# Attention, MLP and gated MLP on one core: each engine's queue laid down by the kernel's own list scheduler

## The chip, the cores and the metric

The kernel runs on one core of one Trainium2 chip. The metric is the time of one execution on the device in microseconds; what is reported is the median of several runs.

## What is computed

Sparse attention in which each query keeps its 32 largest scores, then an MLP with SiLU, then a gated product with two more matrices. In the reference:

```python
scores = scale * np.matmul(q, k.transpose(0, 1, 3, 2))          # 4 x 8 heads, 576 x 576, head_dim 64
kth = np.partition(scores, -top_k, axis=-1)[..., -top_k:-top_k + 1]   # top_k = 32
scores = np.where(scores >= kth, scores, -1000000000.0)
attn = softmax(scores)                                          # max subtracted, sum + 1e-9
x = (attn @ v) as 2304 tokens x 512
h = x @ w_in;  x = (h * sigmoid(h)) @ w_out                     # d_ff 2048
out = ((x @ w1) * (x @ w2)) @ w3 @ w_out2                       # d_ff 1024, out 2304 x 512
```

## The kernel before

The 2304 tokens are cut into 6 blocks of 384 (BLOCKS). Block j has 8 heads of 3 tiles of 128 queries, 24 tiles, which are taken in pairs. For a pair, `plan_scores` makes the scores on TensorE in two halves of 288 columns (L397, L398) and copies them to SBUF on ScalarE (L401). `plan_topk` finds the 32 largest of a row on VectorE by four MAX8 (L428) and three MATCH_REPLACE8 (L432), and masks (L448) and exponentiates (L454) on ScalarE. `plan_av` transposes the probabilities by TensorE (L538, L540; in blocks 0 and 1, which are "native", by a matmul with a diagonal matrix, L535), copies them on ScalarE (L546, L553, L554) and multiplies with v (L566 native, L575). For float32 accuracy at the speed of fp32r, most operands are split into a high part (a ScalarE cast) and a low part (a GpSimd subtraction), and every MLP product is three matmuls (`three`, L637 to L639).

`mlp(j)` has 16 steps of the first MLP (`l1`, `tanh`, `gate`, `split_to`, `l2`), then 8 steps of the gated one (`l3`, `prod`, `l4`, L758). w3 times the last matrix is folded once at the beginning (`fold_steps`, L220 and L225). The weights come as 64-bit numbers; 24 pieces of the fold and 48 of the MLPs are loaded (`convert_load`, L121 and L123), converted by two ScalarE passes (L128, L129), a GpSimd clamp (L132) and a VectorE shift (L137), split (L183, L184) and written to DRAM (L172) while block 0 is computed. Blocks 1 to 5 stream them back (`stream`, L188). The raw pieces have 4 buffers.

The order in which operations are recorded comes from a plan in ticks, 7 of them (SLOT) for each pair, into which `Spread` deals the steps of `mlp(j)`, so that MLP j runs beside attention j+1. The framework then orders the queues by a simulated timeline of its own (`schedule_with_timeline_sim=True`, at the launch), from that recorded order as priority. The eight PSUM banks are eight fixed tiles; `bank` pops one from a list at recording, and `done` puts it back, so that an operation is tied to one bank when it is recorded:

```python
free_banks = [ps_p.tile([128, 512], FP32, name=f"bank{i}") for i in range(8)]
def bank(why=""):
    b = free_banks.pop(0)
    held[id(b)] = why
    return b
```

Of the kernel before, what the change touches and what calls it, by code (L numbers as in the profile page):

```python
# [1 line left out]

# [21 lines left out]
LAG = 1  # L24
WT = 3
# [4 lines left out]
XB = 6  # L30
GB = 2
# [18 lines left out]
TB = 2  # L50


@with_exitstack
def attention_moe_moe2_kernel(
    ctx: ExitStack,
# [9 lines left out]
    w4: bass.AP,  # L65
    out: bass.AP,
):
    nc = tc.nc
    B, H, D2, S = qT.shape
    D = D2 // 2  # L70
    NT, DM = out.shape
# [8 lines left out]
    scale = 1.0 / float(D) ** 0.5  # L80
    NB = len(BLOCKS)

    w4_p = ctx.enter_context(tc.tile_pool(name="w4", bufs=1))
    wt_p = ctx.enter_context(tc.tile_pool(name="wt", bufs=WT))
    raw_p = ctx.enter_context(tc.tile_pool(name="raw", bufs=2))
    x_p = ctx.enter_context(tc.tile_pool(name="x", bufs=XB))
    x2_p = ctx.enter_context(tc.tile_pool(name="x2", bufs=1))
    g_p = ctx.enter_context(tc.tile_pool(name="g", bufs=GB + LAG))
    kv_p = ctx.enter_context(tc.tile_pool(name="kv", bufs=2))
    s_p = ctx.enter_context(tc.tile_pool(name="s", bufs=2))  # L90
    pt_p = ctx.enter_context(tc.tile_pool(name="pt", bufs=2))
    ps_p = ctx.enter_context(tc.tile_pool(name="ps", bufs=1, space=bass.MemoryType.PSUM))
    dram = ctx.enter_context(tc.tile_pool(name="dram", bufs=1, space=bass.MemoryType.DRAM))


    free_banks = [ps_p.tile([128, 512], FP32, name=f"bank{i}") for i in range(8)]

    held = {}

    def bank(why=""):  # L100
        if not free_banks:
            raise RuntimeError(f"no bank: {sorted(held.values())}")
        b = free_banks.pop(0)
        held[id(b)] = why
        return b

    def done(b):
        held.pop(id(b))
        free_banks.append(b)
# [80 lines left out]
    def fold_steps():  # L190
# [89 lines left out]
    ready = [0] * NB  # L280
# [97 lines left out]
    def plan_scores(n, base):  # L378
# [9 lines left out]
        def go(tick, j, h, i, half, si, r0, r1):  # L388
            hd = heads[j, h]
            if n not in tiles:  # L390
                tiles[n] = s_p.tile([128, 2, S], FP32, tag="st", bufs=SB, name="st")
            m = pairs[n].index((j, h, i))
            kk = hd["k"][si][0]
            ps = bank("s")
            cs = slice(half * HS, (half + 1) * HS)
            q_ = hd["q"][:, i * 128:(i + 1) * 128]
            nc.tensor.matmul(ps[:, 0:HS], lhsT=q_, rhs=kk[:, 0, cs], start=True, stop=False)  # L397
            nc.tensor.matmul(ps[:, 0:HS], lhsT=q_, rhs=kk[:, 1, cs], start=False, stop=True)  # L398

# [103 lines left out]
    def plan_av(j, h):  # L503
# [22 lines left out]
        for kc in range(KC):  # L526
            u = {}

            def tr(u=u, kc=kc):
                u["ps"] = ps = bank("pt")  # L530
                for i in range(BLOCKS[j]):
                    p = st["p"][i]
                    if native:
                        kn = REM if kc == NFULL else 128
                        nc.tensor.matmul(ps[0:kn, i * 128:(i + 1) * 128], lhsT=p[:, kc * 128:kc * 128 + kn],  # L535
                                         rhs=st["d"][:, i * 128:(i + 1) * 128], start=True, stop=True)
                    elif kc < NFULL:
                        nc.tensor.transpose(ps[:, i * 128:(i + 1) * 128], p[:, kc * 128:kc * 128 + 128], ident)  # L538
                    else:
                        nc.tensor.transpose(ps[:, i * 128:(i + 1) * 128], p[:, kc * 128:kc * 128 + 128], ident)  # L540

            def ev(u=u, kc=kc):
                if native:
                    kn = REM if kc == NFULL else 128
                    pf = pt_p.tile([128, T], FP32, tag="ph", bufs=3, name="pn")
                    nc.scalar.copy(out=pf[0:kn], in_=u["ps"][0:kn, 0:T])  # L546
                    done(u["ps"])
                    u["m"] = pf
                    return
# [264 lines left out]
            self.i = len(self.todo)  # L814

    with ExitStack():
        make_identity(nc, ident)
        nc.gpsimd.memset(sums, 1e-9)
        nc.gpsimd.memset(low, 7.5 * 2.0 ** -16 - 0.5)
        start = min(plan)  # L820
        fs = fold_steps() + [f for k in range(8) for f in (lambda k=k: conv_step(k), lambda: None)]
        side = Spread(fs, ready[0] - RO)
        j = -1
        tick = start
        while plan or j + 1 < NB:
            todo = plan.pop(tick, [])
            while todo:
                todo.sort(key=lambda x: x[:2])
                todo.pop(0)[2]()
                todo += plan.pop(tick, [])  # L830
            if tick >= FS:
                side.tick()
            if j + 1 < NB and tick == ready[j + 1]:
                side.rest()
                j += 1
                side = Spread(mlp(j), ready[j + 1] - ready[j] - MO if j + 1 < NB else 1)
            tick += 1
        side.rest()


# [42 lines left out]
```

## Time and profile before

| | |
|---|---|
| median of 3 runs | 1192.65 us (1192.61 to 1194.92) |
| profiled execution | 1192.3 us, span 1190.2 us |
| instructions | 19686 |
| TensorE busy, matmuls | 1114.8 us (94%) |
| TensorE busy, weight loads | 994.6 us (84%) |
| VectorE, ScalarE, GpSimd busy | 905.4, 860.0, 712.9 us |
| DMA | 273.53 MB, 230 GB/s |
| mean granted TensorE clock | 0.974 |

Busy time is the union of an engine's instructions. TensorE's matmuls overlap one another in the record, so its share says less than that of the other engines. In the tables below, PE is TensorE's matmuls, PEld its weight loads, DVE VectorE, ACT ScalarE, POOL GpSimd, SP the engine whose queue issues most DMAs; L12 is line 12 of the kernel.

### The profile page before, as it was taken

The numbers are of one execution on the slowest core, as the hardware profiler recorded it, in microseconds if no ns is written. First come the engines' busy times: TensorE is split into PE (matmuls) and PEld (weight loads), VectorE is DVE, ScalarE is ACT, GpSimd is POOL, SyncE is SP. The second block draws the span as 40 slices with busy tenths as digits, with TensorE's granted clock in tenths as the row PEclk, the third lists the DMA queues.
The fourth block names the chain that finished last, engine by engine and source line by source line (L and its number), as shares of the span: only waits on it lengthen the run. The fifth ranks groups of instructions, "written<-read, shape, count | busy, mean of one in ns | idle before, by whom it ended". The sixth has DMA issues, their size and how long they took to land.

```text
span 1190.2 us, 19686 instructions
## 1 busy us (share of the span) xinstructions
PE 1114.8 (94%) x6216; PEld 994.6 (84%) x6216; DVE 905.4 (76%) x2112; ACT 860.0 (72%) x1931; POOL 712.9 (60%) x744
## 2 busy tenths in 40 slices
PE   5899958989789999999999999999999999999998
PEld 2454547888679899999899999999999999999997
DVE  6999899787857888999889987887799899601100
ACT  6896888888887587887778877877868778642221
POOL 4443465777767366786677866767855766542231
PEclk8999978999889999999999999999999999999999
DMA  9965395786978567756688776889757774538640
GB/s 295 323 205 167 105 319 170 273 308 233 313 254 273 205 219 242 227 201 236 204 249 277 239 243 206 282 281 316 249 200 227 231 249 154 188 113 284 243 166 26
DMA packets 127879, 273.53 MB, mean 230 GB/s; under 512 B 40480, under 2 KB 65056, under 8 KB 127776
## 3 DMA queue, kind: packets, MB, share of 16 engines
q1 hardware_dynamic: 119712, 245.02, 62.7%
q10 hardware_dynamic: 8064, 27.27, 6.0%
q8 instruction: 49, 0.80, 0.3%
q14 instruction: 54, 0.44, 0.1%
HBM read 216.14 MB, written 56.10 MB: 229 GB/s over the span
## 4 chain that ended last, share of the span: by engine, by line
PE 68%; ACT 11%; DVE 10%; DMA 6%; issue 3%; POOL 3%; SPq 0%; ACTq 0%; POOLq 0%; DVEq 0%
PE bank L637 14%; PE bank L638 14%; PE bank L639 13%; PE bank L758 8%; DVE top L428 4%; PE bank L575 4%; DVE wk L432 3%; PE bank L538 3%; DMA raw<-in_w_dram 3%; PE bank L397 2%; PE bank L566 2%; PE bank L398 2%; PE bank L535 2%; PE bank L220 2%; DVE w L137 2%
## 5 line engine op out<-in xcount | busy, mean ns | idle before, releaser
L428 DVE MAX8 top<-wk 128x8 f32<-128x576 f32 x432 | 320.3, 752 | 5.2
L652 POOL TENSOR_TENSOR gl<-gf,gh 128x384 fp32r<-128x384 f32 x144 | 148.9, 1036 | 139.6 <-ACT gh L651 138.4
L432 DVE MATCH_REPLACE8 wk<-top,wk 128x576 f32<-128x576 f32 x288 | 213.2, 742 | 0.0
L556 POOL TENSOR_TENSOR pl<-pf,ph 128x384 fp32r<-128x384 f32 x128 | 129.5, 1020 | 78.1 <-ACT ph L554 69.4
L401 ACT ACTIVATE st<-bank 128x288 f32<-128x288 f32 (+1 forms) x320 | 127.8, 415 | 32.4 <-PE bank L398 29.9
L428 DVE MAX8 top<-st 128x8 f32<-128x576 f32 x144 | 108.0, 751 | 46.5 <-ACT st L401 46.0
L637 PE MATMUL bank<-x2h,wt 128*128 128x384 f32 x384 | 131.5, 346 | 6.1 <-ACT x2h L696 4.6
L638 PE MATMUL bank<-gl,wt 128*128 128x384 f32 x384 | 132.3, 344 | 1.7 <-POOL gl L652 1.2
L637 PE MATMUL bank<-xh,wt 128*128 128x384 f32 x384 | 131.0, 344 | 2.9 <-DVE gf L679 2.0
L638 PE MATMUL bank<-x2l,wt 128*128 128x384 f32 x384 | 130.2, 339 | 1.1 <-POOL x2l L697 0.9
L639 PE MATMUL bank<-gh,wt 128*128 128x384 f32 x384 | 130.2, 339 | 0.0
L639 PE MATMUL bank<-xh,wt 128*128 128x384 f32 x384 | 129.9, 338 | 0.0
L638 PE MATMUL bank<-xl,wt 128*128 128x384 f32 x384 | 129.8, 338 | 0.0
L639 PE MATMUL bank<-x2h,wt 128*128 128x384 f32 x384 | 129.3, 337 | 0.0
L397 PE MATMUL bank<-kk,qs 128*128 128x288 f32 x320 | 108.3, 350 | 18.3 <-POOL qs L320 5.1
L679 DVE SCALAR_TENSOR_TENSOR gf<-th,bank 128x384 f32<-128x384 f32 x96 | 52.2, 549 | 88.3 <-ACT th L674 84.3
L448 ACT ACTIVATE e<-st,nt 128x576 f32<-128x576 f32 x144 | 105.1, 775 | 14.1 <-DVE nt L440 12.9
L454 ACT ACTIVATE e<-e,nb 128x576 f32<-128x576 f32 x144 | 112.0, 780 | 0.1
L651 ACT CAST gh<-gf 128x384 fp32r<-128x384 f32 x144 | 74.1, 516 | 49.6 <-DVE gf L746 33.0
L432 DVE MATCH_REPLACE8 wk<-top,st 128x576 f32<-128x576 f32 x144 | 106.7, 742 | 0.0
L553 ACT COPY pf<-bank 128x384 f32<-128x384 f32 (+1 forms) x160 | 77.3, 483 | 32.5 <-PE bank L538 20.5
L132 POOL TENSOR_SCALAR t<-t 128x512 int16<-128x512 int16 x72 | 59.1, 820 | 67.8 <-ACT t L128 58.2
(90 smaller groups left out, 2924.3 us busy)
## 6 DMA issues: line engine op xcount, KB each, us to landing
wt<-scr SPq DMA_DIRECT2D x240, 512.0 KB, 4.3
scr<-wt ACTq DMA_DIRECT2D x48, 512.0 KB, 5.4
k<-kk SPq DMA_DIRECT2D x32, 576.0 KB, 5.2
kk<-k SPq DMA_DIRECT2D x32, 576.0 KB, 5.1
raw<-in_w_dram SPq DMA_DIRECT2D x24, 512.0 KB, 5.6
kr<-in_kT_dram SPq DMA_DIRECT2D x32, 288.0 KB, 5.5
raw<-in_w3T_dram SPq DMA_DIRECT2D x16, 512.0 KB, 5.2
raw<-in_w_in_dram SPq DMA_DIRECT2D x16, 512.0 KB, 5.2
```

Of the source, the lines that this page charges most:

```text
L397: nc.tensor.matmul(ps[:, 0:HS], lhsT=q_, rhs=kk[:, 0, cs], start=True, stop=False)
L401: nc.scalar.activation(out=tiles[n][r0:r1, m, cs], in_=ps[r0:r1, 0:HS], func=ACTF.Copy, scale=scale)
L428: nc.vector.max(out=st["top"][:, i, r * 8:r * 8 + 8], in_=st["s" if r == 0 else "wk"][:, i])
L432: nc.vector.match_replace(out=st["wk"][:, i], in_to_replace=st["top"][:, i, r * 8:r * 8 + 8], in_values=st["s" if r == 0 else "wk"][:, i], ...
L448: nc.scalar.activation(out=e[:, 0:S], in_=st["s"][:, i], func=ACTF.Prelu, bias=st["nt"][:, i:i + 1], alpha=BELOW)
L454: nc.scalar.activation(out=e, in_=e, func=ACTF.Exp, bias=st["nb"][:, i:i + 1], accum_out=st["sm"][:, i, 0:1])
L556: nc.gpsimd.tensor_sub(out=pl[f], in0=pf[f], in1=ph[f])
L637: nc.tensor.matmul(ps, lhsT=wh, rhs=rh, start=first, stop=False)
L638: nc.tensor.matmul(ps, lhsT=wh, rhs=rl, start=False, stop=False)
L639: nc.tensor.matmul(ps, lhsT=wl, rhs=rh, start=False, stop=last)
L652: nc.gpsimd.tensor_sub(out=u["l"], in0=full, in1=u["h"])
L758: nc.tensor.matmul(oacc[t], lhsT=a[:, ts], rhs=b[:, i, :], start=(i == 0 and x == 0), stop=(i == NI - 1 and x == 2))
```

## The change

Pools and engines are wrapped. A call of an engine, `nc.scalar.copy(...)`, makes an `Op` that holds the engine, the arguments and two durations from `cost()`: how long it holds its engine, and when its result is there. `Recorder.add` finds what it depends on by the regions that it reads and writes. `Recorder.schedule` then plays the whole program: each engine takes the operation that can start first, and of those that are ready the one recorded first; a tile is given a buffer of its pool in the recorded order of first use, when one is free. DMAs share one modelled wire. `emit` makes the real calls in the order of the starts found, inside `tc.manual_schedule()`, in which the framework keeps the order of each queue and only sets the semaphores. The PSUM banks become one pool tag with 8 buffers; `done` does nothing. The operations, the plan in ticks and all sizes stay.

```diff
+    def cost(self):
+        n = max(columns(x) for x in self.ins + self.outs)
+        if self.dma:
...
+            return (70 if self.engine == "sync" else 230), size / (375. if run >= 2048 else 310. if run >= 1024 else 260.)
+        if self.engine == "tensor":
+            m = columns(self.ins[-1])
+            if self.ins[0].dtype == FP32R:
+                t = m / 2.4 * 13 / 12
+            else:
+                t = 108 if self.name == "transpose" else m / 0.6 + (44 if columns(self.ins[0]) < 128 else 4)
+            return t, t + 165
+        if self.engine == "vector":
+            t = n / 0.96 + 61
...
+            return t, t + 90
+        if self.engine == "gpsimd":
...
+                t = n * 2.45 + 30
+            return t, t + 45
+        t = n / 0.96 + (-30 if self.name == "copy" else 110 if self.ins[0].dtype == U32 else 60)
+        return t + (92 if "accum_out" in self.kw else 0), t + (200 if "accum_out" in self.kw else 112)
...
+        def offer(n):
+            o = ops[n]
+            for t in o.takes:
+                if t in reserved:
+                    continue
+                if given.get(t.key, 0) != turn[t] or not spare[t.key]:
+                    parked.setdefault(t.key, []).append(n)
+                    return
...
+        for _ in ops:
+            best = None
+            for e in ready:
+                if ready[e] or later[e]:
+                    t = free[e] if ready[e] else max(free[e], later[e][0][0])
+                    if best is None or t < best[0]:
+                        best = t, e
+            t, e = best
+            while later[e] and later[e][0][0] <= t:
+                heapq.heappush(ready[e], heapq.heappop(later[e])[1])
+            n = heapq.heappop(ready[e])
+            o = ops[n]
+            start[n] = t
+            free[e] = t + o.hold
+            end = t + o.done
+            if o.dma:
+                wire = max(wire, t + 1600) + o.done
+                end = wire + 1200
...
+        return [ops[n] for n in sorted(range(len(ops)), key=lambda n: (start[n], n))]
+
+    def emit(self):
+        for o in self.schedule():
+            o.call(*[real_ap(x) for x in o.args], **{k: real_ap(x) for k, x in o.kw.items()})
...
-    nc = tc.nc
+    real = tc.nc
+    nc = Recorder(real)
...
     def bank(why=""):
-        if not free_banks:
-            raise RuntimeError(f"no bank: {sorted(held.values())}")
-        b = free_banks.pop(0)
-        held[id(b)] = why
-        return b
+        return ps_p.tile([128, 512], FP32, tag="bank", bufs=8, name="bank")
...
+    with tc.manual_schedule():
+        nc.emit()
```

## Rows read from the trace of the kernel before

**Rows 1.** The page: busy time by engine, and the span in 40 slices.
```profile
PE 1114.8 (94%) x6216; PEld 994.6 (84%) x6216; DVE 905.4 (76%) x2112; ACT 860.0 (72%) x1931; POOL 712.9 (60%) x744
...
PE   5899958989789999999999999999999999999998
...
PEclk8999978999889999999999999999999999999999
...
GB/s 295 323 205 167 105 319 170 273 308 233 313 254 273 205 219 242 227 201 236 204 249 277 239 243 206 282 281 316 249 200 227 231 249 154 188 113 284 243 166 26
```

**Rows 2.** Busy time by stage: PE, PEld, DVE, ACT, POOL, then clock, DMA share, GB/s.
```profile
0.00:187.40 187.40, 149.22 (x582) 85.89 (x583) 170.84 (x386) 151.27 (x321) 85.07 (x101) 0.92 0.69 227
187.40:422.00 234.60, 212.76 (x1188) 187.37 (x1187) 180.48 (x387) 180.61 (x379) 153.82 (x154) 0.95 0.76 258
422.00:582.00 160.00, 158.41 (x941) 152.00 (x940) 143.10 (x350) 129.12 (x304) 117.32 (x122) 1.00 0.69 222
582.00:746.00 164.00, 161.43 (x956) 155.35 (x955) 144.50 (x348) 128.92 (x304) 116.81 (x121) 0.99 0.74 242
746.00:911.00 165.00, 162.74 (x1014) 155.61 (x1013) 141.31 (x348) 131.13 (x310) 115.40 (x120) 1.00 0.78 262
911.00:1070.00 159.00, 156.21 (x921) 149.22 (x919) 112.02 (x274) 109.72 (x258) 96.28 (x101) 1.00 0.57 191
1070.00:1190.00 120.00, 114.06 (x626) 109.15 (x624) 13.15 (x24) 29.16 (x61) 28.24 (x28) 0.99 0.52 180
```

**Rows 3.** The chain that ended last: shares, and pieces of it (start, us, what).
```profile
PE 68%; ACT 11%; DVE 10%; DMA 6%; issue 3%; POOL 3%; SPq 0%; ACTq 0%; POOLq 0%; DVEq 0%
...
57.39 0.13 PE bank L397
...
63.80 2.58 PE bank L535 x22
...
106.09 2.08 PE bank L566 x6
...
572.69 2.10 PE bank L758 x9
...
789.73 0.33 PE bank L538 x3
790.32 0.69 PE bank L637 x4
```

**Rows 4.** Groups of instructions by line: one of nine alike on TensorE.
```profile
L637 PE MATMUL bank<-xh,wt 128*128 128x384 f32 x384 | 131.0, 344 | 2.9 <-DVE gf L679 2.0 <-ACT pn L546 0.5
```

**Rows 5.** VectorE's waits, 0 to 187.4 us: total, times, longest.
```profile
DVE w L137 <- POOL t L132: 9.3, 1, 9.3
DVE top L428 <- ACT st L401: 4.4, 4, 2.8
```

**Rows 6.** Waits of ScalarE and VectorE, 187.4 to 422 us.
```profile
ACT raw L129 <- DMA raw<-in_w_dram: 8.2, 6, 2.4
ACT st L401 <- PE bank L398: 5.6, 10, 1.0
ACT raw L129 <- DMA raw<-in_w_out_dram: 5.2, 3, 2.5
...
ACT raw L129 <- DMA raw<-in_w_in_dram: 2.7, 3, 1.9
...
DVE top L428 <- ACT st L401: 18.0, 7, 8.2
```

**Rows 7.** Instructions in order of time, near 300 us.
```profile
298.48 0.74 ACT L129 ACTIVATE raw<-raw,low 128x512 int32<-128x512 uint32 x1 [2.39 <-DMA raw<-in_w_dram]
...
301.05 0.40 PE L397 MATMUL bank<-kk,qs 128*128 128x288 f32 x1 [2.26 <-ACT st L401]
```

**Rows 8.** DMA issues: queue, count, KB each, median us from issue to landing.
```profile
wt<-scr SPq DMA_DIRECT2D x240, 512.0 KB, 4.3
...
raw<-in_w_dram SPq DMA_DIRECT2D x24, 512.0 KB, 5.6
```

More of the change, by code (lines that the diff above doesn't have):

```diff
@@ L1 @@
+import heapq
 from contextlib import ExitStack
@@ L4 @@
 import concourse.tile as tile
+from concourse import bacc
 from concourse import mybir
@@ L50, with __init__, __getattr__, __getitem__ @@
 TB = 2
+class View:
+    def __init__(self, tile, ap, path):
+        self.tile, self.ap_, self.path = tile, ap, path
+    def __getattr__(self, name):
+        got = getattr(self.ap_, name)
+        if not callable(got):
+            return got
+        return lambda *a, **k: View(self.tile, got(*a, **k), self.path + [(name, a, k)])
+    def __getitem__(self, key):
+        return View(self.tile, self.ap_[key], self.path + [("__getitem__", (key,), {})])
+SHADOW = []
+def template(shape, dtype):
+    if not SHADOW:
+        SHADOW.append((bacc.Bacc("TRN2", target_bir_lowering=False, num_devices=1), {}))
+    nc, known = SHADOW[0]
+    key = tuple(shape), str(dtype)
+    if key not in known:
+        known[key] = nc.dram_tensor(f"shape_{len(known)}", list(shape), dtype, kind="Internal").ap()
+    return known[key]
@@ new lines, with __init__, is_ap, base @@
+class Slotted:
+    def __init__(self, key, make):
+        self.key, self.make, self.made = key, make, None
+def is_ap(x):
+    return isinstance(x, (bass.AP, View))
+def base(ap):
+    return ap.tile if isinstance(ap, View) else ap.tensor.name
+def real_ap(x):
+    if not isinstance(x, View):
+        return x
+    t = x.tile
+    if t.made is None:
+        t.made = t.make()
+    ap = t.made
+    for name, a, k in x.path:
+        ap = getattr(ap, name)(*a, **k)
+    return ap
+def columns(ap):
+    n = 1
+    for _, c in ap.ap[1:]:
+        n *= c
+    return n
@@ new lines, with __init__, __getattr__, pool @@
+class Recorder:
+    def __init__(self, nc):
+        self.ops, self.seen, self.first, self.caps = [], {}, {}, {}
+        for e in ("sync", "scalar", "vector", "gpsimd", "tensor"):
+            setattr(self, e, Recorder.Engine(self, e, getattr(nc, e)))
+    class Engine:
+        def __init__(self, rec, name, real):
+            self.rec, self.name, self.real = rec, name, real
+        def __getattr__(self, fn):
+            return lambda *a, **k: self.rec.add(Op(self.name, getattr(self.real, fn), fn, a, k))
+    def pool(self, pool, name, bufs):
+        return Recorder.Pool(self, pool, name, bufs)
+    class Pool:
+        def __init__(self, rec, pool, name, bufs):
+            self.rec, self.real, self.name, self.bufs = rec, pool, name, bufs
+        def tile(self, shape, dtype, tag=None, bufs=None, name=None):
+            if tag is None:
+                return self.real.tile(shape, dtype, name=name)
+            key = self.name, tag
+            self.rec.caps[key] = bufs or self.bufs
+            t = Slotted(key, lambda: self.real.tile(shape, dtype, tag=tag, bufs=bufs or self.bufs, name=name))
+            return View(t, template(shape, dtype), [])
+    def add(self, op):
+        n = len(self.ops)
+        self.ops.append(op)
+        acc = [(x, False) for x in op.ins] + [(x, True) for x in op.outs]
+        for ap, write in acc:
+            t = base(ap)
+            log = self.seen.setdefault(t, [])
+            r = region(ap)
+            for q, k, w in log:
+                if (write or w) and k != n and meets(q, r):
+                    op.needs.add(k)
+            if isinstance(t, Slotted):
+                op.tiles[t] = True
+                if t not in self.first:
+                    self.first[t] = n
+                    op.takes.append(t)
+                elif self.first[t] != n:
+                    op.weak.add(self.first[t])
+        op.weak -= op.needs
+        for ap, write in acc:
+            log, r = self.seen[base(ap)], region(ap)
+            if write:
+                log[:] = [x for x in log if x[1] == n or not covers(r, x[0])]
+            log.append((r, n, write))
+    def schedule(self):
+        ops = self.ops
+        left, heirs, weak = [len(o.needs) + len(o.weak) for o in ops], [[] for _ in ops], [[] for _ in ops]
+        users, ahead, turn = {}, {}, {}
+        for n, o in enumerate(ops):
+            for k in sorted(o.needs):
+                heirs[k].append(n)
+            for k in sorted(o.weak):
+                weak[k].append(n)
+            for t in o.tiles:
+                users[t] = users.get(t, 0) + 1
+            for t in o.takes:
+                turn[t] = ahead[t.key] = ahead.get(t.key, -1) + 1
+        spare = {k: [(0., c) for c in range(v)] for k, v in self.caps.items()}
+        given, lastuse, parked = {}, {}, {}
+        avail, start = [0.] * len(ops), [0.] * len(ops)
+        ready = {e: [] for e in ("sync", "scalar", "vector", "gpsimd", "tensor")}
+        later = {e: [] for e in ready}
+        free = dict.fromkeys(ready, 0.)
+        wire = 0.
+        reserved = {}
+        def offer(n):
+            o = ops[n]
+            for t in o.takes:
+                if t in reserved:
[3 more added lines that the diff above has]
+                    return
+            for t in o.takes:
+                if t not in reserved:
+                    reserved[t] = heapq.heappop(spare[t.key])
+                    given[t.key] = given.get(t.key, 0) + 1
+                avail[n] = max(avail[n], reserved[t][0])
+            heapq.heappush(later[o.engine], (avail[n], n))
+            for t in o.takes:
+                wake(t.key)
+        def wake(key):
+            for n in parked.pop(key, []):
+                offer(n)
+        for n in range(len(ops)):
+            if not left[n]:
+                offer(n)
+        for _ in ops:
[16 more added lines that the diff above has]
+                end = wire + 1200
+            for x in o.tiles:
+                users[x] -= 1
+                lastuse[x] = max(lastuse.get(x, 0.), end + 45)
+                if not users[x]:
+                    heapq.heappush(spare[x.key], (lastuse[x], reserved[x][1]))
+                    wake(x.key)
+            for k in heirs[n]:
+                left[k] -= 1
+                same = e == "tensor" and ops[k].engine == e
+                avail[k] = max(avail[k], free[e] if same else end + 45)
+                if not left[k]:
+                    offer(k)
+            for k in weak[n]:
+                left[k] -= 1
+                if not left[k]:
+                    offer(k)
+        return [ops[n] for n in sorted(range(len(ops)), key=lambda n: (start[n], n))]
+    def emit(self):
+        for o in self.schedule():
+            o.call(*[real_ap(x) for x in o.args], **{k: real_ap(x) for k, x in o.kw.items()})
@@ L816, in attention_moe_moe2_kernel @@
     with ExitStack():
-        make_identity(nc, ident)
-        nc.gpsimd.memset(sums, 1e-9)
-        nc.gpsimd.memset(low, 7.5 * 2.0 ** -16 - 0.5)
+        make_identity(real, ident)
+        real.gpsimd.memset(sums, 1e-9)
+        real.gpsimd.memset(low, 7.5 * 2.0 ** -16 - 0.5)
         start = min(plan)
```

61 lines of the change are left out of this document (46 added, 15 removed).

## The prediction

> **What bounds the kernel now.** I read the whole first: how busy each engine is and the slices [rows 1]. TensorE (PE) is busy for 1114.8 of 1190.2 us, but by slices it is short of work in the first third and the throttle grants 1.2 of 2.4 GHz in parts of it. So I cut the span where the outputs show that one stage hands over to the next [rows 2]. Stage A (0 to 187.4) is the attention of block 0 with the folding of w3 and w4, before the first MLP matmul. Stage B (to 422) is MLP 0 beside attention 1, and the conversion of the MLP weights. Stage C (422 to 1070) has four alike stages, MLP j beside attention j+1. Stage D is MLP 5 alone.
>
> In A, VectorE (DVE) sets the pace: 170.84 of 187.4 us busy. Its idle time has a wait of 9.3 us for the first converted weights, at the start, and 4.4 us for scores [rows 5]. In C and D, PE sets it: 156 to 163 us busy in stages of 159 to 165. In B nothing is full: PE 212.76, ScalarE (ACT) 180.61, DVE 180.48 of 234.6 us, DMA share 0.76, granted clock 0.95.
>
> A matmul's recorded length overlaps the next (mean 344 ns, [rows 4]), so I count PE's need by the distance from start to start in the dense pieces of the chain [rows 3]: 0.69/4 = 0.1725 us for an MLP matmul of 384 columns, 2.10/9 = 0.233 for one of L758, 0.13 for a score matmul, 0.33/3 = 0.11 for a transpose, 2.58/22 = 0.117 for a record of L535, 2.08/6 = 0.347 for one of L566. One block's MLP has 3 x 64 x 3 = 576 matmuls of the first kind and 72 of L758: 99.4 + 16.8 = 116.2 us. A block's scores are about 107 x 0.13 = 14. The attention of blocks 2 to 5 adds 120 transposes (13.2) and 72 products (12.4); block 1, by the native way, adds 240 records of L535 (28.0) and 80 of L566 (27.8). So a C stage needs 116.2 + 14 + 13.2 + 12.4 = 155.8 us and B needs 116.2 + 14 + 28.0 + 27.8 = 186.
>
> The excess: 234.6 - 186 = 48.6 us in B, and 4.2 + 8.2 + 9.2 + 3.2 = 24.8 in C.
>
> The Trainium skill (Perfetto Trace Analysis, Identifying the Most-Contended Engine) says that matmul busy time is a bad measure of how near TensorE is to its limit, and that the weight loads' share is a better one. The trace agrees: 94% against 84% [rows 1], and by the busy time alone the room in B would be 21.8 us, not 48.6. By the page the room is nearer to the last rival's than to the forecast's.
>
> **The change, part by part.** *No work is added or taken away*: the same instructions on the same engines, the same DMAs, shapes and pools. The recording is done before the program runs, so it costs nothing on the chip. What changes is the order in each engine's queue (SP's and ACT's DMAs too), and with it which wait stands at a queue's head.
>
> *The durations.* The new costs stand near the trace: 384/2.4 x 13/12 = 173 ns against 172.5, 512 columns 231 against 233, a transpose 108 against 110. So where engines set the pace, the order laid down should be nearly the order in which things get ready. What such an order can save is a head-of-queue wait with ready work behind it. [rows 7] show one: ACT stands 2.39 us at its head for a weight load and then does the conversion, while PE idles 2.26 us until a score copy (L401) that stands behind it.
>
> *Stage A.* DVE is the limit and its work stays. Of its waits only the 4.4 us for scores can go. Bounds 0 and -4.4; I take -3, since four waits of that kind are just what a better order of L401 on ACT removes.
>
> *Stage B.* Here the queues wait on each other: ACT stands 8.2 + 5.2 + 2.7 = 16.1 us for weight loads and 5.6 for scores, DVE 18.0 for scores [rows 6]. Floors: PE 186; ACT 180.6; DMA 258 GB/s x 234.6 us = 60.5 MB, at the best slice's 323 GB/s [rows 1] 187 us. So the stage can't go below 187: bounds 0 and -47. Three resources that are each 80% full and coupled by four raw buffers won't all fill. I take a third of the excess, -16, since the load waits, 16.1 us, are not cured by an order whose landing times are too short (below).
>
> *Stage C.* Bounds 0 and -24.8. There PE always has accumulations of an open bank to go on with, so the rest is small waits at stage borders. I take half, -12.
>
> *Stage D.* One engine, dense, no choice of order: 0. Its last output is as late as before.
>
> *The banks.* Before, a bank is fixed when the operation is recorded; after, any free one is taken, but strictly in recorded order, so a first matmul that isn't ready keeps back the first matmul of every later tile. No row shows this. The nearest is the PE wait of 2.26 us in [rows 7]: from 0 to 24 such waits (one for each hidden tile of MLP 0), 24 x 2.26 = 54 us. I take 0, because recorded ticks already put consumers a step or more behind producers, and keep the 54 for the range.
>
> *The DMA model.* The new code lets a 512 KB transfer land 1.6 + 512 KB / 375 GB/s (1.4) + 1.2 = 4.2 us after its issue, and frees SP after 0.07 us. Rows: 4.3 us for the streamed weights, 240 of them, which fits, but 5.6 for the largest group of raw loads [rows 8], and no slice moves more than 323 GB/s. So C's streams are placed well and conversions 1.4 us too early. I take 0 beyond the uncured 16.1 us, since raw buffers are refilled ahead; the other end is a rival.
>
> Sum: -3 - 16 - 12 + 0 = -31 us. The profiled execution took 1192.3 us (span 1190.2), beside a median of 1192.65, so the forecast is 1192.3 - 31 = 1161 us.
>
> **Rivals.**
> *Conversions at ACT's head too early (slower).* An L128 or L129 placed 1.4 us before its load lands blocks ACT, and behind it score copies, exps and casts. For it: ACT shows 12 such waits in B already [rows 6]. Against it: with four raw buffers a load usually has a step's time to spare. There are 72 raw loads; if two in three (48) reach the path it costs 48 x 1.4 = 67 us, less the 16 already in the trace: 1161 + 51 = 1212 us. It decides from (31 + 16)/1.4 = 34 of the 72 on.
>
> *The order was as good already (no change).* The framework also orders by a simulated timeline, and B's excess would be the weight cycle itself (load, two ACT passes, POOL, DVE, cast, subtract through four buffers), whatever the order. For it: the chain has 6% DMA and 10% DVE [rows 3], each step waiting for data and not behind a queue. Against it: [rows 7]. It leaves only A's -3: 1189 us, or 1192 without it.
>
> *The early stages close up (much faster).* B goes to 195 us (-40), C loses 20 of its 24.8, A all 4.4 and some 6 more if top-k goes ahead of conversions that MLP 0 needs only later: -70, 1122 us. For it: the granted clock of 0.92 and 0.95 in A and B [rows 2], which a PE with fewer gaps gets back. Against it: B has three resources near 187 us.
>
> **How the numbers follow.** Forecast (1140 to 1184 us) 0.50; early stages close up 0.15; no change 0.10; conversions too early, or banks kept back, 0.25. Faster by over 0.2% (2.4 us, about what a measurement of this kernel tells from no change): 0.50 + 0.15 + 0.03 of the no-change case = 0.68; same 0.07; slower 0.25. The likeliest gives 1161. Range 1124 to 1208: about 0.07 lies below it (most of the last rival's better half) and about 0.10 above (the slower rival's worse part, up to 1161 + 54 = 1215 by the banks).
>
> **What would show it.** Right: the first MLP matmul still near 184 us, B near 219, C's four stages near 159 each, D still 120, and ACT's waits for raw loads in B still near 16 us. Wrong: ACT's raw waits above 40 us in B (the slower rival); the first MLP matmul later than 195, which would mean conversions or banks hold back attention 0; B under 200 (the last rival); D longer, if MLP 5 begins with its streamed weights or attention late. The forecast fails most easily in B, where the term of 16 us is a share and not a count.

## The result, and the profile after

| | before | after |
|---|---|---|
| median | 1193.79 us (4 runs) | 1173.25 us (4 runs, 1170.69 to 1173.89) |
| ratio of the times | | 0.9824 [0.9804, 0.9844] |
| profiled execution, its span | 1192.3, 1190.2 us | 1170.69, 1168.9 us |
| mean granted TensorE clock | 0.974 | 0.987 |

The kernel became faster by 1.8%. The forecast was 1161 us with a range of 1124 to 1208: sign and range hold, and about a third of the forecast gain is missing. The sum of the forecast is made up of stages, so the spans are cut into stages once more. I put the borders at the same events in both traces: the first MLP matmul (A to B), and then the first output DMA of each block.

| stage | before | after | difference | forecast |
|---|---|---|---|---|
| A, attention 0 and fold | 187.4 | 178.1 | -9.3 | -3 |
| B, MLP 0 beside attention 1 | 234.7 | 232.9 | -1.8 | -16 |
| C, four stages | 647.7 | 634.2 | -13.5 | -12 |
| D, MLP 5 alone | 120.4 | 123.7 | +3.3 | 0 |
| span | 1190.2 | 1168.9 | -21.3 | -31 |

These differences depend in part on the border. Before, the first matmul of an MLP comes 3.8 us (MLP 1) and 5.9 us (MLP 5) ahead of the output DMA that I took as border; after, it comes 1.1 and 0.6 us behind it. With these first matmuls as borders, A is the same, B is 230.9 before and 234.0 after (+3.1), C 645.6 and 633.7 (-11.9), D 126.3 and 123.1 (-3.2). So what B gave lies between -1.8 and +3.1 us.

The page after, which answers to [rows 1] and to the first row of [rows 3]: busy time of each engine, the slices of TensorE, of its clock and of the DMA rate, the chain's shares.

```profile
PE 1108.4 (95%) x6216; PEld 989.2 (85%) x6216; DVE 898.8 (77%) x2112; ACT 871.0 (75%) x1931; POOL 715.3 (61%) x744
...
PE   4899987989799999999999999999999999999998
...
PEclk9899988999999999999999999999999999999999
...
GB/s 239 262 264 199 104 228 282 287 345 283 321 257 294 144 227 242 250 201 217 226 264 270 231 249 225 270 327 284 265 205 232 256 219 211 133 154 258 252 155 28
...
PE 74%; ACT 9%; POOL 4%; DMA 4%; DVE 4%; issue 3%; SPq 1%; ACTq 0%; POOLq 0%; DVEq 0%
```

The instruction counts of the engines are those of before, and no work has left: the gain is order. In both kernels TensorE is short of work only in the first third. VectorE's share of the chain fell from 10% to 4%, and GpSimd's rose from 3% to 4%.

The windows of after by its own stages, columns as in [rows 2]:

```profile
0.00:178.10 178.10, 149.44 (x577) 85.74 (x577) 159.22 (x367) 140.43 (x297) 75.40 (x89) 0.95 0.68 217
178.10:410.90 232.80, 207.89 (x1168) 177.51 (x1168) 188.95 (x403) 192.50 (x400) 167.07 (x165) 0.98 0.83 277
410.90:569.60 158.70, 158.09 (x942) 152.86 (x942) 142.56 (x349) 130.20 (x303) 115.46 (x121) 1.00 0.69 224
569.60:727.50 157.90, 157.37 (x943) 152.37 (x942) 139.07 (x344) 130.80 (x304) 115.72 (x121) 1.00 0.75 247
727.50:892.20 164.70, 164.70 (x1039) 159.68 (x1038) 143.60 (x354) 134.31 (x314) 117.70 (x122) 1.00 0.79 267
892.20:1045.10 152.90, 152.35 (x907) 147.42 (x906) 112.06 (x276) 112.50 (x258) 94.80 (x100) 1.00 0.60 200
1045.10:1168.90 123.80, 118.59 (x652) 113.58 (x650) 13.33 (x24) 30.25 (x62) 29.16 (x29) 0.99 0.54 175
```

Read A and B together. In A VectorE is busy for 159.22 us where it was 170.84, with 367 instructions where it had 386; ScalarE has 10.8 us less and GpSimd 9.7 less. In B they have 8.5, 11.9 and 13.3 us more. So A got shorter by passing work on, and B did that work in about the same time as before. TensorE did a little less in B, 1168 matmuls against 1189: 17 of MLP 1 came ahead of the border before, and none does after. It stood idle in B for 24.9 us (before 21.8). In C TensorE is busy all but 0.6, 0.5, 0.0 and 0.6 us of a stage; before it was 1.6 to 2.8 us short of each.

In the new kernel all scheduled instructions are emitted at one line, L313, so waits are read by tile. First VectorE's waits in A (they answer to [rows 5]), in a second fence some of the waits of all engines in B (they answer to [rows 6]), in a third TensorE's in C.

```profile
DVE w L313 <- POOL t L313: 8.3, 1, 8.3
DVE top L313 <- ACT st L313: 5.7, 3, 5.0
```

```profile
DVE w L313 <- POOL t L313: 13.8, 13, 3.5
...
PE bank L313 <- POOL dg L313: 10.9, 5, 8.0
ACT raw L313 <- POOL wt L313: 8.9, 7, 2.0
...
DVE top L313 <- ACT st L313: 7.8, 7, 4.7
...
PE bank L313 <- POOL gl L313: 4.6, 2, 2.6
...
PE bank L313 <- ACT gh L313: 4.2, 3, 1.4
...
ACT st L313 <- PE bank L313: 3.0, 4, 1.0
...
ACT gh L313 <- POOL wt L313: 2.4, 1, 2.4
```

```profile
PE bank L313 <- POOL gl L313: 1.3, 4, 0.4
```

In A the wait for scores didn't go: 5.7 us where it was 4.4. In B ScalarE no longer waits for a raw load at all; before that was 16.1 us. Its longest waits now end on `wt`, a GpSimd subtraction that reads the cast weights: 8.9 + 2.4 us, with two smaller ones 13.1 us in ten stops, where before there was none. VectorE's wait for scores fell from 18.0 to 7.8, and in its place it waits 13.8 us for `t`, GpSimd's clamp in the conversion (before 1.5). TensorE waits 10.9 us for `dg`, the diagonal matrix that GpSimd makes for the native attention; none of its waits in B ended on `dg` before. Much of what was a wait for DMA and ScalarE became a wait for GpSimd. In C, 1.3 us is all that TensorE waits for another engine.

The pass `raw<-raw,low` doesn't read `wt`. One of the ten stops in order of time shows what holds it:

```profile
257.62 0.69 DVE L313 SCALAR_TENSOR_TENSOR w<-t,raw 128x512 uint32<-128x512 uint32 x1 [3.27 <-POOL t L313]
257.67 1.77 POOL L313 TENSOR_TENSOR wt<-w,wt 128x512 fp32r<-128x512 f32 x1
...
259.47 0.33 ACTq L313 DMA_DIRECT2D scr<-wt  x1
259.84 0.76 ACT L313 ACTIVATE raw<-raw,low 128x512 int32<-128x512 uint32 x1 [2.03 <-POOL wt L313]
```

In all ten the instruction just ahead in ScalarE's queue is the issue of `scr<-wt`, which writes a converted piece to DRAM and needs the subtraction's result. So the waits for loads at ScalarE's head were replaced by waits of its own DMA issues, again with ready work behind them.

### The profile page after: what moved, and what is told of

The parts are those of the page before. It is cut to its first block, busy times and chain, and to the rows that moved or that the text cites. A ratio compares the mean times of both kernels' runs of the same rounds, so it can differ in the third digit from the quotient of the medians.

```text
span 1168.9 us, 19832 instructions
## 1 busy us (share of the span) xinstructions
PE 1108.4 (95%) x6216; PEld 989.2 (85%) x6216; DVE 898.8 (77%) x2112; ACT 871.0 (75%) x1931; POOL 715.3 (61%) x744
## 4 chain that ended last, share of the span: by engine, by line
PE 74%; ACT 9%; POOL 4%; DMA 4%; DVE 4%; issue 3%; SPq 1%; ACTq 0%; POOLq 0%; DVEq 0%
PE bank L313 74%; ACT e L313 3%; DVE top L313 1%; DVE wk L313 1%; DMA vn<-in_v_dram 1%; ACT st L313 1%; POOL gl L313 1%; DVE w L313 1%; ACT raw L313 1%; ACT t L313 1%; SPq L313 1%; POOL wt L313 1%; DMA k<-kk 0%; DMA raw<-in_w_out_dram 0%; DMA kr<-in_kT_dram 0%
## 5 line engine op out<-in xcount | busy, mean ns | idle before, releaser
L313 DVE MAX8 top<-wk 128x8 f32<-128x576 f32 x432 | 313.1, 750 | 2.6
L313 POOL TENSOR_TENSOR gl<-gf,gh 128x384 fp32r<-128x384 f32 x144 | 148.1, 1028 | 158.1 <-ACT gh L313 157.6
L313 PE MATMUL bank<-gh,wt 128*128 128x384 f32 x768 | 224.2, 342 | 4.2 <-ACT gh L313 4.2
L313 PE MATMUL bank<-xh,wt 128*128 128x384 f32 x768 | 223.5, 342 | 0.3
L313 PE MATMUL bank<-x2h,wt 128*128 128x384 f32 x768 | 219.8, 341 | 0.0
L313 DVE MATCH_REPLACE8 wk<-top,wk 128x576 f32<-128x576 f32 x288 | 212.9, 742 | 0.0
L313 POOL TENSOR_TENSOR pl<-pf,ph 128x384 fp32r<-128x384 f32 x128 | 129.3, 1017 | 65.8 <-ACT ph L313 56.7
L313 ACT ACTIVATE st<-bank 128x288 f32<-128x288 f32 (+1 forms) x320 | 129.0, 410 | 48.1 <-PE bank L313 45.8
L313 PE MATMUL bank<-kk,qs 128*128 128x288 f32 x640 | 149.0, 322 | 15.9 <-POOL qs L313 8.0
L313 PEld LDWEIGHTS bank<-kk,qs 128*128 128x128 f32 x640 | 116.4, 196 | 39.6 <-issue 14.4
L313 PEld LDWEIGHTS bank<-gh,wt 128*128 128x128 f32 x768 | 140.7, 189 | 7.0 <-ACT gh L313 5.1
L313 PEld LDWEIGHTS bank<-xh,wt 128*128 128x128 f32 x768 | 141.5, 189 | 4.2 <-issue 1.9
L313 PEld LDWEIGHTS bank<-x2h,wt 128*128 128x128 f32 x768 | 140.6, 188 | 4.3 <-issue 2.5
L313 PE MATMUL bank<-gl,wt 128*128 128x384 f32 x384 | 130.3, 339 | 6.1 <-POOL gl L313 5.8
L313 PE MATMUL bank<-xl,wt 128*128 128x384 f32 x384 | 129.6, 338 | 0.0
L313 PE MATMUL bank<-x2l,wt 128*128 128x384 f32 x384 | 129.4, 338 | 0.2
L313 DVE MAX8 top<-st 128x8 f32<-128x576 f32 x144 | 107.5, 750 | 28.4 <-ACT st L313 27.6
L313 ACT ACTIVATE e<-st,nt 128x576 f32<-128x576 f32 x144 | 106.5, 773 | 12.2 <-DVE nt L313 12.0
L313 DVE SCALAR_TENSOR_TENSOR gf<-th,bank 128x384 f32<-128x384 f32 x96 | 52.7, 549 | 77.9 <-ACT th L313 75.4
L313 ACT ACTIVATE e<-e,nb 128x576 f32<-128x576 f32 x144 | 111.3, 775 | 0.1
L313 ACT CAST gh<-gf 128x384 fp32r<-128x384 f32 x144 | 74.2, 515 | 44.3 <-DVE gf L313 41.4
L313 DVE MATCH_REPLACE8 wk<-top,st 128x576 f32<-128x576 f32 x144 | 106.7, 742 | 0.0
```

Source lines behind the costliest of these rows:

```text
L313: o.call(*[real_ap(x) for x in o.args], **{k: real_ap(x) for k, x in o.kw.items()})
```

## The experiments

Ratios are to the kernel before, run on the same chip, with a 95% interval; that of the change itself is 0.9824 [0.9804, 0.9844].

### The banks alone, and the order alone

The change has two parts that can be taken apart: the banks from a pool, and the order laid down. `e1_banks_only` keeps the recorder and the pool of banks, but emits in recorded order and lets the framework order the queues. `e2_fixed_banks` keeps the order laid down and goes back to eight fixed banks.

```diff
 # e1_banks_only
-        for o in self.schedule():
+        for o in self.ops:
...
-    with tc.manual_schedule():
-        nc.emit()
+    nc.emit()
 # e2_fixed_banks
+    free_banks = [ps_p.tile([128, 512], FP32, name=f"bank{i}")[:, :] for i in range(8)]
...
-        return ps_p.tile([128, 512], FP32, tag="bank", bufs=8, name="bank")
+        return free_banks.pop(0)
...
-        pass
+        free_banks.append(b)
```

> The banks are taken from a pool of eight as in the changed kernel, but the operations are called in the recorded order and the framework orders the queues by its own simulated timeline, as before. If the order laid down by the kernel makes the gain (my theory), this stands near the kernel before, 1188 to 1198 us. If the free choice of banks makes it (rival), it stands near the changed kernel, 1170 to 1180 us.

> The changed kernel with the eight fixed banks of the kernel before, chosen at recording. If the order makes the gain, 1166 to 1178 us, like the changed kernel; if the banks do, 1188 us or more. If taking banks strictly in recorded order costs something, it is faster than the changed kernel by some us.

Measured: e1 1224.03 us, 1.0271 [1.0235, 1.0307]; e2 1169.64 us, 0.9806 [0.9776, 0.9836]. e2 came out as expected of the order, e1 slower than either of its two cases. By stages e1 is at A 190.8, B 240.9, C 666.3, D 123.4: it loses most in C (+18.6), where TensorE now waits for ScalarE's cast of the gate. The longest of TensorE's waits of e1 in C:

```profile
PE bank L313 <- ACT gh L313: 19.5, 7, 4.5
```

So the gain is the order's. The pool of banks gives nothing with the order laid down, as e2's interval overlaps the change's; under the framework's order e1 is 2.7% slower than the kernel before. That the banks alone make this is not shown, since in e1 every other tile too is made at its first use and not where the program asks for it. Why the framework orders it worse was not tried.

### Three theories for what B lacks

B was to lose 16 us and lost 1.8. The first theory was that the scheduler's cheap DMAs (0.07 us on SP's queue, 375 GB/s) put transfers in the wrong places; the second that conversions had slipped out of A into B; the third that the engine work of the conversions fills B, whatever the transfers do.

```diff
 # e3_dma_cost
-            return (70 if self.engine == "sync" else 230), size / (375. if run >= 2048 else 310. if run >= 1024 else 260.)
+            return (430 if self.engine == "sync" else 330), size / 310.
...
-                wire = max(wire, t + 1600) + o.done
-                end = wire + 1200
+                wire = max(wire, t + 2000) + o.done
+                end = wire + 1500
 # e5_conv_early: fold and first conversions recorded to end 10 ticks earlier
-RO = 0
+RO = 10
 # e6_no_conv: the 48 MLP pieces
-            conv_st[a] = (conv_st[a], convert_scale(conv_st[a], False))
+            pass
...
-            conv_st[a] = convert_bits(*conv_st[a])
+            pass
...
-            w = conv_st.pop(a)
+            w = conv_st.pop(a)[:, :, 1].bitcast(FP32)
```

> The changed kernel, with other DMA costs in its planner alone: a transfer holds SP for 0.43 us in place of 0.07, runs at 310 GB/s in place of 375, and lands 3.5 us beyond that in place of 2.8. If the queue order of the weight stage (MLP 0 with its conversions) is spoilt by transfers planned too short (my theory), that stage shrinks from 233 us by 10 or more and the whole is 1140 to 1158 us. If the stage is bound by the conversion cycle itself whatever the order (rival), it stays within 5 us of 233 and the whole at 1168 to 1178 us.

> The changed kernel with the fold and the first conversions recorded over ten ticks less (RO 10 in place of 0), so that they stand earlier in the planner's priority. If conversions that slipped from stage A into stage B are what B lost (my theory), the first MLP matmul comes 2 to 5 us later than 178 and B shrinks from 233 us by 5 or more: 1164 to 1171 us. If B is held by something else (rival), B stays within 3 us of 233 and the whole at 1172 to 1178 us.

> The changed kernel without the two ScalarE passes, the GpSimd clamp and the VectorE shift of the 48 MLP pieces; they are loaded, cast, split, written out and streamed as before, from one half of the 64-bit numbers. If the conversion's engine work sets stage B (my theory), B shrinks from 233 us to 195 to 210 and the whole is 1135 to 1150 us. If its transfers or TensorE's own order set it (rival), B stays above 222 and the whole above 1160 us.

Measured: e3 1173.45 us, 0.9842 [0.9814, 0.9869]; e5 1171.27 us, 0.9822 [0.9799, 0.9846]; e6 1141.09 us, 0.9571 [0.9545, 0.9596]. B of e3 is 236.9 (after 232.9), so dearer DMAs in the plan gained nothing. In e5 A is 182.9 (+4.8) and B 231.4 (-1.5), so what A gave up B didn't gain. Both theories fell, though the time of e5 lies just between its two ranges. e6 came out as its theory expected. The window of B in e6:

```profile
173.50:381.10 207.60, 200.59 (x1163) 176.06 (x1162) 151.71 (x358) 140.19 (x307) 116.43 (x119) 0.98 0.86 298
```

Without the two ScalarE passes, the clamp and the shift, B has 25.3 us less (232.9 to 207.6), though all raw pieces are still loaded, and at 298 GB/s. So the transfers alone don't hold B at 233; the passes of the conversions do, by their work or by the chain that they form from engine to engine, which e6 takes out together. 208 is still 22 above the floor of 186 that I had counted for TensorE.

### Which planned durations matter

If the waits now end on GpSimd, its planned durations should matter more than others. `e4_flat_costs` plans GpSimd by the elements at one rate, as the other engines are, and the float32 matmuls at the rate of fp32r; `e7_flat_gpsimd` does the first of these alone.

```diff
 # e4_flat_costs and e7_flat_gpsimd
-            if self.name == "tensor_scalar":
-                t = 775 if self.ins[0].dtype == I16 else n * 1.16 + 30
-            else:
-                t = n * 2.45 + 30
-            return t, t + 45
+            t = n / 0.96 + 61
+            return t, t + 90
 # e4_flat_costs as well
-            if self.ins[0].dtype == FP32R:
-                t = m / 2.4 * 13 / 12
-            else:
-                t = 108 if self.name == "transpose" else m / 0.6 + (44 if columns(self.ins[0]) < 128 else 4)
+            t = m / 2.4 * 13 / 12
```

> The changed kernel with the trace-fitted durations of GpSimd and of the four-byte matmuls taken out of its planner: GpSimd is planned as fast as VectorE (384 columns 0.46 us in place of 0.97), plain float32 matmuls as fast as fp32r (512 columns 0.23 us in place of 0.86). If the fitted durations matter, the gain is lost or more than lost, 1185 to 1215 us. If any list order will do (rival), 1168 to 1180 us.

> The changed kernel with one wrong duration in its planner: GpSimd is planned as fast as VectorE (384 columns 0.46 us in place of 0.97); float32 matmuls stay as fitted. If GpSimd's price is the fitted duration that matters most (my theory), most of the 66 us that the planner lost with both flat comes back here: 1200 to 1235 us. If the float32 matmuls' price did it (rival), 1172 to 1190 us.

Measured: e4 1239.02 us, 1.0391 [1.0359, 1.0423], slower than either case expected; e7 1208.83 us, 1.0129 [1.0101, 1.0158], as its theory had it, though with 35.6 of the 65.8 us that e4 loses on the change GpSimd's price makes little more than half. The stages of e7 stand at A +3.1, B +21.4, C +15.0, D +0.7 against after. The step from e7 to e4 lies in A: 181.2 to 204.7, +23.5, where the fold's float32 matmuls are; B moves by -0.7 and C by +4.4. A of e4, B of e7, and TensorE's waits in B of e7:

```profile
0.00:204.70 204.70, 152.99 (x583) 88.67 (x584) 154.58 (x359) 140.01 (x297) 77.22 (x91) 0.89 0.58 187
```

```profile
181.20:435.50 254.30, 218.88 (x1168) 188.54 (x1168) 192.44 (x404) 192.15 (x402) 163.57 (x165) 0.93 0.77 253
```

```profile
PE bank L310 <- POOL gl L310: 11.9, 7, 2.6
PE bank L310 <- ACT gh L310: 11.3, 4, 5.3
```

The engines' busy times in B are near those of after, VectorE's 192.44 against 188.95, ScalarE's 192.15 against 192.50, but the stage is 21.5 us longer, and all of that is idle time. TensorE waits for `gl`, a GpSimd subtraction, 11.9 us where it waited 4.6. ScalarE's stops that end on `wt` are 23.8 us in e7 and 13.1 in after, nearly all behind an issue of `scr<-wt`: where the plan has the subtraction done too soon, the issue comes too early in ScalarE's queue. An order planned with GpSimd's 512-element subtraction at 0.59 us (512/0.96 + 61 ns) where the trace has 1.30 costs 3% against the change and is slower than the framework's own. Just any order of a list scheduler doesn't do.

### One engine relieved

If one engine held B, to take work off it should shorten B. `e9_clamp_dve` gives the clamps of the 48 MLP pieces to VectorE; `e10_cast_dve` takes the 48 casts off ScalarE.

```diff
 # e9_clamp_dve
-        nc.gpsimd.tensor_scalar(top, top, 32767, FLOOR, op0=ALU.min, op1=ALU.max)
+        (nc.gpsimd if fold else nc.vector).tensor_scalar(top, top, 32767, FLOOR, op0=ALU.min, op1=ALU.max)
 # e10_cast_dve
-            nc.scalar.copy(out=t[:, 0], in_=w)
+            nc.vector.tensor_copy(out=t[:, 0], in_=w)
```

> The changed kernel with the clamp of the 48 MLP pieces (L132, 0.77 us each) on VectorE in place of GpSimd. If GpSimd is the engine of the conversion that holds stage B (theory), B shrinks from 233 us by 8 or more, to 1160 to 1167 us. If ScalarE's passes hold it (rival), B stays within 4 us of 233 and the whole at 1169 to 1178 us.

> The changed kernel with the cast of the 48 converted MLP pieces (L183, 0.61 us each) on VectorE in place of ScalarE. If ScalarE's passes hold stage B (rival of the run beside it), B shrinks from 233 us by 8 or more, to 1160 to 1167 us. If GpSimd holds it, B stays within 4 us of 233 and the whole at 1169 to 1178 us. If neither alone holds it, both runs stay there.

Measured: e9 1171.13 us, 0.981 [0.9769, 0.9851], B 234.4; e10 1173.49 us, 0.9828 [0.9797, 0.986], B 237.4. This is the case that neither alone holds B. The windows of B, of e9 and of e10:

```profile
176.60:411.00 234.40, 212.47 (x1168) 181.30 (x1168) 213.86 (x451) 193.74 (x400) 131.02 (x123) 0.96 0.82 276
```

```profile
174.50:411.90 237.40, 210.93 (x1168) 181.50 (x1168) 222.78 (x454) 172.03 (x355) 170.82 (x165) 0.95 0.80 271
```

GpSimd was relieved of 36 us and ScalarE of 20 us, and B got no shorter. VectorE took on 25 and 34 us, and B got longer by 1.6 and 4.6 us only, though with 222.78 of 237.4 us VectorE is itself near full in e10. So to relieve GpSimd or ScalarE at VectorE's cost doesn't shorten B. No run takes work off VectorE alone, so that VectorE holds B isn't excluded. That the chain from one engine to the next sets B's length is my reading, and is not shown.

### Durations fitted again, and a looser record

The trace of after shows where the planned durations are off: a `dg` of 0.375 us is planned at 0.178 (128 x 1.16 + 30 ns), a clamp planned at 0.775 takes up to 1.25, an issue of a raw load shows a median of 0.33 to 0.38 us on SP's queue and is planned at 0.07. `e12_refit_only` corrects such durations. `e8_refit` has these, fixed banks as in e2, fold and first conversions recorded to end 10 ticks earlier (RO), and the product with v one tick later (AVD). `e11_refit_plan` is e8 with 15 ticks, and with more room in the record: the product another tick later (AVD 4), scores and loads recorded 2 ticks earlier (QL 5).

```diff
 # e12_refit_only, and in e8_refit and e11_refit_plan
-            return (70 if self.engine == "sync" else 230), size / (375. if run >= 2048 else 310. if run >= 1024 else 260.)
+            return (430 if self.engine == "sync" else 365), size / (375. if run >= 2048 else 310. if run >= 1024 else 260.)
...
-                t = 108 if self.name == "transpose" else m / 0.6 + (44 if columns(self.ins[0]) < 128 else 4)
+                t = 108 if self.name == "transpose" else (m / 0.6 + (44 if columns(self.ins[0]) < 128 else 4)) * 1.15
...
-                t += 180
+                t += 255
...
-                t = 775 if self.ins[0].dtype == I16 else n * 1.16 + 30
+                t = 850 if self.ins[0].dtype == I16 else n * 1.16 + 30 if n > 128 else 400
...
-                t = n * 2.45 + 30
+                t = n * 2.45 + (140 if n == 512 or self.outs[0].ap[0][1] == 64 else 40)
...
-        t = n / 0.96 + (-30 if self.name == "copy" else 110 if self.ins[0].dtype == U32 else 60)
-        return t + (92 if "accum_out" in self.kw else 0), t + (200 if "accum_out" in self.kw else 112)
+        t = n / 0.96 + (-30 if self.name == "copy" else 110 if self.ins[0].dtype == U32 else -10 if n < 512 else 60)
+        return t + (92 if "accum_out" in self.kw else 0), t + (200 if "accum_out" in self.kw else 120)
...
-                lastuse[x] = max(lastuse.get(x, 0.), end + 45)
+                lastuse[x] = max(lastuse.get(x, 0.), end + 90)
...
-                avail[k] = max(avail[k], free[e] if same else end + 45)
+                avail[k] = max(avail[k], free[e] if same else end + 90)
 # e8_refit as well, beside the fixed banks of e2
-AVD = 2
+AVD = 3
...
-RO = 0
+RO = 10
 # e11_refit_plan instead
-AVD = 2
+AVD = 4
...
-RO = 0
+RO = 15
...
-QL = 3
+QL = 5
```

> The changed kernel with durations fitted again to its own trace (GpSimd clamp 0.85 us, diagonal 0.40, subtractions after a wait 0.1 longer, VectorE shift 0.85, float32 matmuls 15% longer, ScalarE's short activations 0.07 shorter, DMA issue 0.43 and 0.365, 90 ns from end to start), the eight fixed banks, RO 10 and the products two ticks after their transposes put to three (AVD). If small durations in the planner are what holds back A and B (my theory), 1150 to 1162 us. If the plan's order is no longer what sets them (rival), 1164 to 1174 us.

> The refitted planner with the eight fixed banks (the run e8_refit), and its plan in ticks loosened further: RO 15, AVD 4, and scores two ticks earlier (QL 5). If room between the recorded steps is what the planner lacks (theory), 1155 to 1162 us. If the refitted kernel is already at what this plan can give (rival), 1162 to 1168 us.

> The changed kernel with the refitted durations of e8_refit alone; banks from the pool, RO 0 and AVD 2 as in the change. If the refitted durations made the 9 us that e8_refit gained on the change (theory), 1163 to 1167 us. If the fixed banks, RO and AVD made it (rival), 1170 to 1175 us.

Measured: e8 1164.4 us, 0.9762 [0.9741, 0.9784]; e11 1160.22 us, 0.9737 [0.9709, 0.9764]; e12 1168.0 us, 0.9805 [0.978, 0.9831]. The intervals of e8 and e11 lie apart from the change's, so both beat both kernels; between the two the intervals overlap. e12 overlaps the change's and is inconclusive by itself. e8 lies at the lower end of its rival's range, e11 in its theory's, e12 between its two. B of e8, and A and B of e11:

```profile
176.20:405.30 229.10, 210.78 (x1163) 180.16 (x1162) 196.74 (x411) 188.80 (x394) 162.38 (x161) 0.96 0.83 274
```

```profile
0.00:182.20 182.20, 150.92 (x588) 85.27 (x589) 167.10 (x376) 145.04 (x312) 82.49 (x97) 0.93 0.70 228
182.20:401.00 218.80, 205.85 (x1164) 179.20 (x1163) 190.78 (x409) 188.58 (x395) 162.49 (x160) 0.98 0.83 281
```

TensorE's waits in B of e11:

```profile
PE bank L313 <- POOL gl L313: 4.0, 3, 1.9
PE bank L313 <- POOL dg L313: 3.9, 1, 3.9
```

In e11 all engines have about the work in B that they have after (VectorE 190.78 against 188.95, ScalarE 188.58 against 192.50) and do it in 218.8 us; the wait for `dg` is 3.9 us instead of 10.9, and ScalarE's stops that end on `wt` are 3.4 us instead of 13.1. A is 4.1 us longer than after. B of e12 is 229.5 and of e8 229.1, so in these traces the durations alone bring what e8 has in B; the step to 218.7 comes with the looser record of e11 (RO, AVD and QL together), and 6.0 of its 10.4 us come back in A, which is 176.2 in e8. Which of the three edits carries it was not separated.

## Why the prediction held, and where it didn't

**No work added or taken away.** Right: the engines' instructions are the same in number, and e2 shows that the order makes the gain without the pool of banks.

**Stage A, -3 forecast, -9.3 measured.** That VectorE sets the pace held: it is busy for 159.22 of 178.1 us. "Its work stays" is the step that failed, and with it the lower bound of -4.4. VectorE's conversion shifts before the first MLP matmul fell from 33 to 30 and its MAX8 from 115 to 109, so less of block 1's top-k came before it; the last MAX8 of block 0 ends at 157.2 instead of 163.3 us. VectorE's idle time in A even grew, from 16.6 to 18.9 us, and the wait for scores that I had called curable is 5.7 us. This is near the mechanism of the last rival (top-k ahead of conversions that MLP 0 needs only later), for which I had estimated some 6 us; what of the 9.3 us comes from the shifts and what from the top-k was not tried.

**Stage B, -16 forecast, -1.8 measured (+3.1 by the first matmuls).** This is the term that was mis-sized, as the prediction said it might. Two of its reasons fell. ScalarE's 16.1 us for raw loads, which I called "not cured", are gone, and B didn't shorten with them: waits on GpSimd took their place, at ScalarE's head behind its own issues of `scr<-wt`. And B didn't do its old work: it did 8.5 to 13.3 us more on each of three engines. A and B together are the fairer account: -19 forecast, -11.1 measured (-6.2 by the first matmuls), and -21.2 in e11 (182.2 + 218.7 against 422.1). So a B of 219 can be had by order, but not by the durations and the record of this change. Two terms of the floors need a word: in B the trace of before has 160 records of L566 of half the columns, 1.77/10 = 0.18 us each, and not 80, which comes to the same 28 us; and a slice of after moves 345 GB/s, so 187 us was no floor of the DMA. That the transfers alone hold B fell by e6, that their planned cost does by e3, that slipped conversions do by e5, that GpSimd or ScalarE alone does by e9 and e10; that the planned GpSimd durations matter is shown by e7. ScalarE's stops that end on `wt` are most where B is longest (23.8 us in e7, B 254.3) and fewest where it is shortest (1.9 in e12, 2.8 in e8, 3.4 in e11). But B of e11 is 10.8 us shorter than that of e12 at about the same stops, so they are at most a part, and no run moves these issues to another queue. What exactly held B back in the change stays open.

**Stage C, -12 forecast, -13.5 measured (-11.9 by the first matmuls).** Right in size and, in the main, in mechanism. That half of the excess would go was a guess that came out. I took half of the 24.8 us above TensorE's counted need; the windows say why there is no more: TensorE is busy for all but 0.6 us of a stage or less. A stage now takes 634.2/4 = 158.6 us on the average, so little was left of the 2.8 us above my count of 155.8.

**Stage D, 0 forecast, +3.3 measured.** A border effect: before, MLP 5's first matmul came 5.9 us ahead of the border, at 1063.9 against 1069.8; after, it comes 0.6 behind it, at 1045.7 against 1045.1. From that matmul to the end it is -3.2. C and D together are -10.2 (forecast -12).

**Banks and DMA model, 0 each.** Right in the order laid down: fixed banks (e2) and dearer DMAs (e3) change nothing that can be measured. The bound of +54 for the banks was far off there; e1 loses 32 us where the framework orders the pool.

**The rivals.** Conversions that block ScalarE's head before their loads land (1212) didn't come: there is no wait for raw loads at ScalarE in B. What blocks the head there is the write at the other end of the conversion. "As good already" (1189 to 1192) fell by the result. "Early stages close up" (1122) holds for A alone.

The sum, then, by the table's borders: A gave 6.3 us more than forecast, C 1.5 more, B 14.2 less and D 3.3 less; 1161 becomes 1170.7, the profiled execution. That the total lies as near as 10 us is in part luck, since A's miss makes up for some of B's.

## What to carry to other kernels

A list scheduler is worth its durations: fit first what is far slower than the common rate (here GpSimd's instructions, and the float32 matmuls on TensorE), because wrong prices there cost more than the scheduler gained. It still goes by the recorded order as priority, so look at both; here the best time came with both changed. A DMA issue waits in its engine's queue like any other instruction, so look at what stands behind it. When a wait goes and the stage stays as long, look for the wait that took its place, and cut the windows at events, so that work that moved over a border is seen; try a second event before you believe a difference of a few microseconds.

## What the runs showed of the hardware

VectorE's shift `w<-t,raw` reads two operands from SBUF. The list of tile `w` in after (duration ns min/median/max) gives its spread beside that of GpSimd's subtraction:

```profile
L313 DVE SCALAR_TENSOR_TENSOR w<-t,raw x72: 665/693/1762, 8.3 to 368.7; 128x512 uint32<-128x512 uint32 x72
...
L313 POOL TENSOR_TENSOR wt<-w,wt x48: 1265/1296/1813, 160.5 to 372.5; 128x512 fp32r<-128x512 f32 x48
```

The same list of tile `top`:

```profile
L313 DVE MAX8 top<-wk x432: 731/750/765, 11.7 to 1011.6; 128x8 f32<-128x576 f32 x144
```

The same shift alone, and with a GpSimd subtraction at work, in order of time, in two stretches of after:

```profile
264.39 0.69 DVE L313 SCALAR_TENSOR_TENSOR w<-t,raw 128x512 uint32<-128x512 uint32 x1 [0.48 <-POOL t L313]
```

```profile
284.47 2.54 POOL L313 TENSOR_TENSOR wt<-w,wt 128x512 fp32r<-128x512 f32 x2
...
285.80 1.76 DVE L313 SCALAR_TENSOR_TENSOR w<-t,raw 128x512 uint32<-128x512 uint32 x1
```

The second of the two subtractions begins near 285.7 (287.01 - 1.30) and ends at 287.01; the shift that starts at 285.80 takes 1.76 us instead of 0.69, about what is left of the subtraction (1.21) and then its own time (together 1.90). All twelve shifts of over 1.3 us in after start within 0.5 us after a GpSimd subtraction has. It goes the other way round too: the thirteen subtractions `wt<-w,wt` of over 1.7 us, in place of 1.30, all start while a shift is at work, like the one at 257.67 above, 0.05 us behind the shift at 257.62. These 432 MAX8, which read one operand, take 731 to 765 ns. The Trainium skill (GPSIMD Engine Reference, Key points) says that GpSimd shares its SBUF interfaces with VectorE, and that VectorE instructions with two SBUF inputs contend with it. By that rule a shift and a subtraction can hold each other up; the trace agrees, with 1.76 against 0.69 us for the one and 1.77 against 1.30 for the other. That the later of the two waits is what these rows show. A planner with one duration for each instruction can't see this: the shift is planned at 0.77 us (512/0.96 + 61 + 180 ns), between the two.
